# Moving the two-input elementwise work of the last token blocks from GpSimd to VectorE, with two of each eight unit pairs multiplied plainly

## The chip, the cores and the metric

The kernel runs on one core of a Trainium2 chip. The metric is the device time of one execution in microseconds (us). TensorE (PE in the profile, PEld for its weight loads) multiplies, VectorE (DVE), ScalarE (ACT) and GpSimd (POOL) work elementwise, and SyncE (SP) issues most transfers.

## The reference, cut to what matters

The first part is a spectral mixing of `x` (4 sequences of 3008 positions, 256 channels): a real FFT along the sequence, a complex 256x256 product with bias, a soft threshold, and the inverse FFT. Its 12032 rows of 256 values then go through a feed-forward network with 2048 hidden units:

```python
def _moe_ref(x, w_in, w_out, alpha):
    h = x @ w_in
    g = np.maximum(h, 0.0) + alpha * np.minimum(h, 0.0)
    return (g @ w_out).astype(np.float32)
```

The change concerns only the feed-forward network on the last 3072 of the 12032 rows, and the preparation of its weights.

## The kernel before, in words

Each fp32 operand of a matmul is split into two parts, `hi` (rounded, made by ScalarE) and `lo` (the rest, `x - hi`, made by VectorE or GpSimd), and each product is three matmuls: hi·hi, lo·hi, hi·lo. TensorE's order is the order of the program; so is that of every other engine (`manual_schedule`).

The first 24 chunks of up to 384 tokens go through the main loop, `l1_step` and `l2_step`, one hidden block of 128 units at a time; the second-layer product of a step is issued `LAG` = 3 steps behind its first-layer product. The last 3072 tokens are six blocks (`NS2` = 6) of `SC` = 512 tokens. Their hidden units go in `PR` = 8 pairs of 128-unit blocks, so there are 48 steps. Step k issues the first layer of pair k (`s_l1`) and then the second layer of pair k-2 (`s_l2`, `SLAG` = 2).

`s_l1` makes the two hidden blocks of the pair, 6 matmuls of 512 columns each, in two buffers of `ps_h`; ScalarE takes the Relu of the negative (`sq`), and a VectorE instruction, scalar_tensor_tensor, completes the activation from `sq` and `ps_h` and so frees the `ps_h` buffer.

In five of the six blocks `s_l2` replaces the 2x2 block product of a pair (two unit blocks x two token halves against two unit blocks x two channel halves, 8 products) by seven products of sums. It needs sums of the activations (`t`), with their `hi` (`h`) and `lo` (`l`) parts, those of the plain quarters (`dh`, `dl`, three quarters in one 768-element instruction), and sums of the output weights (`sw_a`, `sw_b`), which `w_full`, `w_sums` and `w_split` prepare during the last 28 main steps. Seven products accumulate over the eight pairs in three PSUM tiles `a`, `b`, `c` and in `o_last`; `s_out` combines them after the eighth pair, and `s_turn` transposes and stores. The sixth block is multiplied plainly (`z_parts`, `z_l2`, 8 products).

Work tiles rotate over two buffers by tag, so a `dh` of pair k can be written only when TensorE has read that of pair k-2, and the two `ps_o` tiles and `o_last` of a block must be emptied by `s_out` before the next block's first `s_l2` may write them. Between some steps `s_dmm` (16 matmuls, L611) and `s_dpart` (ScalarE and VectorE splits of its result, L139 and L142) make the input rows of the next block.

Of the kernel before, what the change touches and what calls it, by code (L numbers as in the profile page):

```python
# [9 lines left out]
F32 = mybir.dt.float32  # L10
F32R = mybir.dt.float32r
# [82 lines left out]
def fft_mix_moe(ctx, tc, x, w_r, w_i, b_r, b_i, w_in, w_out, alpha, la, rb, lc, rd, lf, cf, sel, out):  # L94
# [38 lines left out]
    def f(t):  # L133
        return t.bitcast(F32)
# [202 lines left out]
    xt = {}  # L337
# [401 lines left out]
    def w_full(p):  # L739

        h, m = divmod(4 * p, FH)
        w = wo_h[h][:, m:m + 4]
        t = work.tile([128, 4, C], F32, tag="xt", name="wo_f")
        G.tensor_tensor(out=t, in0=f(w[:, :, 0]), in1=f(w[:, :, 1]), op=ALU.add)
        wf.append(t)

    def w_sums(p):

        t = wf.pop().rearrange("p (r j) (c h) -> p j h r c", j=2, h=2)
        s = work.tile([128, 4, 2, 128], F32, tag="xt", name="wo_s")  # L750
        G.tensor_tensor(out=s[:, 0], in0=t[:, 0, 1], in1=t[:, 1, 1], op=ALU.add)
        G.tensor_tensor(out=s[:, 1], in0=s[:, 0], in1=t[:, 0, 0], op=ALU.subtract)
        G.tensor_tensor(out=s[:, 2], in0=t[:, 0, 0], in1=t[:, 0, 1], op=ALU.subtract)
        G.tensor_tensor(out=s[:, 3], in0=t[:, 1, 0], in1=s[:, 1], op=ALU.subtract)
        wf.append(s)

    def w_split(p):
        s = wf.pop()
        a, b = (t[:, :, 2 * p:2 * p + 2] for t in sw["all"])
        A.activation(out=a[:, 0:4], in_=s, func=AF.Copy)  # L760
        V.tensor_tensor(out=a[:, 4:6], in0=s[:, 0:2], in1=f(a[:, 0:2]), op=ALU.subtract)
        V.tensor_tensor(out=b, in0=s[:, 2:4], in1=f(a[:, 2:4]), op=ALU.subtract)
# [4 lines left out]
    def s_l1(n, t):  # L767
        yh, yl = yt[CC + n]
        q = work.tile([128, 2, SC], F32, tag="xt", name="sq")
        for j in range(2):  # L770
            m = 2 * t + j
            ps = ps_h.tile([128, SC], F32, tag="h", name="ps_h")
            k = 0
            for ct in range(CT):
                for w, a in ((0, yh), (0, yl), (1, yh)):
                    PE.matmul(ps, wi_h[m // FH][:, w, ct, 128 * (m % FH):128 * (m % FH) + 128], a[:, ct],  # L776
                              start=(k == 0), stop=(k == 3 * CT - 1))
                    k += 1
            A.activation(out=q[:, j], in_=ps, func=AF.Relu, scale=-1.0)
            V.scalar_tensor_tensor(out=q[:, j], in0=q[:, j], scalar=beta_s[:, m:m + 1], in1=ps,  # L780
                                   op0=ALU.mult, op1=ALU.add)
        if n == NS2 - 1:
            z_parts(t, q)
            return
        q = q.rearrange("p j n -> p (j n)")
        b12, b11, b22, b21 = (q[:, HS * k:HS * k + HS] for k in range(4))
        dh = work.tile([128, 3 * HS], F32R, tag="Xh", name="dh")
        dl = work.tile([128, 3 * HS], F32R, tag="Xl", name="dl")
        t3 = work.tile([128, 2, HS], F32, tag="zst", name="t3")
        t1 = work.tile([128, 2, HS], F32, tag="bt", name="t1", bufs=3)  # L790
        h3 = work.tile([128, 2, HS], F32R, tag="xh", name="h3")
        l3 = work.tile([128, 2, HS], F32R, tag="Yh", name="l3")
        h1 = work.tile([128, 2, HS], F32R, tag="xl", name="h1")
        l1 = work.tile([128, 2, HS], F32R, tag="Yl", name="l1")
        A.activation(out=dh, in_=q[:, HS:], func=AF.Copy)  # L795
        V.tensor_tensor(out=t3[:, 0], in0=b22, in1=b12, op=ALU.subtract)
        V.tensor_tensor(out=t3[:, 1], in0=t3[:, 0], in1=b11, op=ALU.add)
        G.tensor_tensor(out=dl, in0=q[:, HS:], in1=f(dh), op=ALU.subtract)  # L798
        for k, b in enumerate((b22, b21)):
            V.tensor_tensor(out=t1[:, k], in0=b, in1=t3[:, 1], op=ALU.subtract)  # L800
        A.activation(out=h3, in_=t3, func=AF.Copy)
        A.activation(out=h1, in_=t1, func=AF.Copy)
# [49 lines left out]
    def s_l2(n, t):  # L852
        if t == 0:
            sa[n] = [ps_o.tile([128, 2, HS], F32, tag="o", name="ps_o") for _ in range(2)] \
                + [ps_f.tile([128, 2, HS], F32, tag="f", name="ps_o")]
        a, b, c = sa[n]
        b11, b22, b21, t3, t2, t1, t4 = sg.pop((n, t))
        r, z = t == 0, t == PR - 1

        def block(j, h):  # L860
            m = 2 * t + j
            w = wo_h[m // FH][:, m % FH].rearrange("p w (c h) -> p w h c", h=2)
            return w[:, 0, h], w[:, 1, h]

        s1, s2, s3, s4 = ([x[:, t] for x in sw[k]] for k in range(4))
        prods = [(block(0, 0), b11, a[:, 0], r, False), (block(1, 0), b21, a[:, 1], False, z),
                 (s4, b22, b[:, 0], r, False), (s3, t3, b[:, 1], False, z),
                 (s2, t2, c[:, 0], r, False), (s1, t1, c[:, 1], False, z),
                 (block(1, 1), t4, o_last[:, 0], r, z)]
        for (wh, wl), (gh, gl), o, first, last in prods:  # L870
            PE.matmul(o, wh, gh, start=first, stop=False)
            PE.matmul(o, wl, gh, start=False, stop=False)
            PE.matmul(o, wh, gl, start=False, stop=last)

    so = {}

    def s_out(n):
        a, b, c = sa.pop(n)
        e = [work.tile([128, HS], F32, tag="q", name="se", bufs=3) for _ in range(3)]
        u = [work.tile([128, HS], F32, tag="gh", name="su", bufs=4) for _ in range(3)]  # L880
        c1 = work.tile([128, 2, HS], F32, tag="Yt", name="c1", bufs=1)
        c2 = work.tile([128, 2, HS], F32, tag="Yc", name="c2", bufs=1)
        A.activation(out=e[0], in_=a[:, 0], func=AF.Copy)
        A.activation(out=e[1], in_=b[:, 0], func=AF.Copy)
        A.activation(out=e[2], in_=c[:, 1], func=AF.Copy)
        V.tensor_tensor(out=c1[:, 1], in0=a[:, 1], in1=e[0], op=ALU.add)
        V.tensor_tensor(out=u[0], in0=c[:, 0], in1=e[0], op=ALU.add)
        V.tensor_tensor(out=u[1], in0=b[:, 1], in1=u[0], op=ALU.add)
        V.tensor_tensor(out=c2[:, 1], in0=o_last[:, 0], in1=u[1], op=ALU.add)
        G.tensor_tensor(out=u[2], in0=u[0], in1=e[2], op=ALU.add)  # L890
        G.tensor_tensor(out=c1[:, 0], in0=u[2], in1=e[1], op=ALU.add)
        G.tensor_tensor(out=c2[:, 0], in0=u[1], in1=e[2], op=ALU.add)
        so[n] = c1, c2

    def s_turn(n):
# [55 lines left out]
    with tc.manual_schedule():  # L951
# [100 lines left out]
        def at(i, fn, *args, when=todo):  # L1052
            when.setdefault(i, []).append((fn, args))
# [157 lines left out]
```

## Time and profile before

| quantity | value |
|---|---|
| median of three runs | 1458.29 us (1456.98 to 1461.1) |
| the profiled execution's own time | 1457.62 us |
| its span, first to last instruction | 1455.8 us |
| mean granted TensorE clock | 0.985 of 2.4 GHz |
| busy over the span: TensorE, VectorE, ScalarE, GpSimd | 96%, 64%, 51%, 37% |

The shares are means over stages with different limits. TensorE is busy all of 200 to 1000 us; from about 1115 to 1411 us, where the five seven-product blocks are computed, it is not. A busy time in the trace counts an instruction that holds its engine while it waits for a memory port.

### The profile page before, as it was taken

What the parts mean: (1) busy time and instruction counts of PE and PEld (TensorE: products, weight loads), DVE (VectorE), ACT (ScalarE), POOL (GpSimd) and SP (SyncE); (2) the same over time, 40 slices, a digit from 0 to 9 for tenths busy, and PEclk for the clock granted to TensorE, in tenths of its full rate; (3) what the DMA queues carried; (4) which work ended last, traced back from release to release, by engine and by line L of the source; (5) the groups of instructions that cost most, each with busy time, mean ns of one, the idle gap of its engine ahead of it and who ended that gap; (6) DMA issues with size and microseconds to landing.
All of it is one profiled execution on the core that took longest, in us unless ns stands there. A gap on an engine that the chain in (4) does not pass through costs nothing.

```text
span 1455.8 us, 25407 instructions
## 1 busy us (share of the span) xinstructions
PE 1391.5 (96%) x9640; PEld 1325.2 (91%) x9640; DVE 929.7 (64%) x1579; ACT 738.0 (51%) x1528; POOL 533.0 (37%) x539
## 2 busy tenths in 40 slices
PE   8999999999999999999999999999998888788898
PEld 5979999999999999999999999999988777677788
DVE  2758756666644446666665566656565888888874
ACT  3556554455455654544466554444545444444453
POOL 4855722223221222222212222232463554454551
PEclk9999999999999999999999999999999999999999
DMA  9954131110112321111223210111010001101001
GB/s 237 247 166 138 55 105 59 59 52 30 52 41 75 88 80 44 40 50 51 73 80 108 63 47 27 59 53 51 30 31 16 21 1 37 25 2 26 6 10 30
DMA packets 72452, 89.68 MB, mean 62 GB/s; under 512 B 22043, under 2 KB 54782, under 8 KB 72329
## 3 DMA queue, kind: packets, MB, share of 16 engines
q1 hardware_dynamic: 63743, 76.74, 18.0%
q0 software_dynamic: 5168, 8.02, 2.1%
q10 hardware_dynamic: 3418, 3.29, 0.7%
q8 instruction: 76, 1.25, 0.4%
q14 instruction: 47, 0.39, 0.1%
HBM read 50.49 MB, written 34.34 MB: 58 GB/s over the span
## 4 chain that ended last, share of the span: by engine, by line
PE 78%; DVE 13%; ACT 4%; issue 3%; DMA 1%; POOL 0%; SPq 0%; ACTq 0%; DVEq 0%; POOLq 0%
PE ps_h L672 25%; PE ps_o L710 6%; PE ps_o L711 6%; PE ps_o L709 6%; PE ps_m L486 5%; PE ps_h L776 5%; PE ps_b L426 3%; DVE t L800 3%; PE o_last L711 3%; PE ps_d L611 3%; PE o_last L709 3%; PE o_last L710 3%; DVE sq L780 3%; PE ps_m L473 3%; DVE l L804 2%
## 5 line engine op out<-in xcount | busy, mean ns | idle before, releaser
L672 PE MATMUL ps_h<-yh,w 128*128 128x384 f32 (+1 forms) x1472 | 431.5, 335 | 4.2 <-DVE q L679 4.1
L684 POOL TENSOR_TENSOR gl<-q,gh 128x384 fp32r<-128x384 f32 (+1 forms) x187 | 193.2, 1033 | 577.1 <-ACT gh L683 527.0
L679 DVE SCALAR_TENSOR_TENSOR q<-q,beta_s,ps_h 128x384 f32<-128x384 f32 (+1 forms) x384 | 230.8, 601 | 234.4 <-ACT q L678 232.3
L683 ACT ACTIVATE gh<-q 128x384 fp32r<-128x384 f32 (+1 forms) x384 | 198.3, 516 | 276.0 <-DVE q L679 272.4
L672 PEld LDWEIGHTS ps_h<-yh,w 128*128 128x128 f32 x1472 | 271.1, 189 | 8.2 <-DVE q L679 4.8
L672 PE MATMUL ps_h<-yl,w 128*128 128x384 f32 (+1 forms) x736 | 243.5, 331 | 0.0
L678 ACT ACTIVATE q<-ps_h 128x384 f32<-128x384 f32 (+1 forms) x384 | 182.5, 475 | 117.9 <-PE ps_h L672 103.0
L711 PE MATMUL ps_o<-w,gl 128*128 128x256 f32 x768 | 216.4, 282 | 3.0 <-POOL gl L684 3.0
L710 PE MATMUL ps_o<-w,gh 128*128 128x256 f32 x768 | 216.9, 282 | 0.0
L709 PE MATMUL ps_o<-w,gh 128*128 128x256 f32 x768 | 216.1, 281 | 0.0
L776 PE MATMUL ps_h<-yh,w 128*128 128x512 f32 x384 | 138.1, 422 | 35.3 <-DVE sq L780 35.3
L684 DVE TENSOR_TENSOR gl<-q,gh 128x384 fp32r<-128x384 f32 (+1 forms) x197 | 120.5, 612 | 66.4 <-ACT gh L683 62.7
L711 PEld LDWEIGHTS ps_o<-w,gl 128*128 128x128 f32 x768 | 146.0, 190 | 3.9 <-POOL gl L684 3.7
L710 PEld LDWEIGHTS ps_o<-w,gh 128*128 128x128 f32 x768 | 145.9, 190 | 0.0
L709 PEld LDWEIGHTS ps_o<-w,gh 128*128 128x128 f32 x768 | 144.7, 188 | 0.0
L672 PEld LDWEIGHTS ps_h<-yl,w 128*128 128x128 f32 x736 | 139.3, 189 | 1.4
L798 POOL TENSOR_TENSOR dl<-sq,dh 128x768 fp32r<-128x768 f32 x40 | 82.2, 2056 | 136.0 <-ACT dh L795 101.4
L776 PEld LDWEIGHTS ps_h<-yh,w 128*128 128x128 f32 x384 | 77.5, 202 | 56.0 <-DVE sq L780 39.8
L711 PE MATMUL o_last<-w,gl 128*128 128x256 f32 x352 | 100.7, 286 | 0.0
L709 PE MATMUL o_last<-w,gh 128*128 128x256 f32 x352 | 100.3, 285 | 0.0
L710 PE MATMUL o_last<-w,gh 128*128 128x256 f32 x352 | 100.3, 285 | 0.0
L800 DVE TENSOR_TENSOR t<-sq,t 128x256 f32<-128x256 f32 x80 | 99.2, 1281 | 1.4
(194 smaller groups left out, 2840.4 us busy)
## 6 DMA issues: line engine op xcount, KB each, us to landing
zt<-zd SPq DMA_DIRECT2D x32, 384.0 KB
ad<-ast SPq DMA_DIRECT2D x48, 192.0 KB
bt<-ad SPq DMA_DIRECT2D x72, 128.0 KB
zd<-zst SPq DMA_DIRECT2D x36, 256.0 KB
xt<-in_x SPq DMA_DIRECT2D x21, 320.0 KB
cw_s<-in_moe_w_in SPq DMA_DIRECT2D x8, 512.0 KB
cw_s<-in_moe_w_out SPq DMA_DIRECT2D x8, 512.0 KB
out<-os SPq DMA_DIRECT2D x26, 128.0 KB
```

Source lines behind the costliest of these rows:

```text
L486: PE.matmul(p, a[:, k:k + 128], mix[i][:, w, ct], start=(n == 0), stop=(n == 3 * CT - 1))
L672: PE.matmul(ps, wi_h[m // FH][:, w, ct, 128 * (m % FH):128 * (m % FH) + 128], a[:, ct, 0:n], start=(k == 0), stop=(k == 3 * CT - 1))
L678: A.activation(out=q, in_=ps, func=AF.Relu, scale=-1.0)
L679: V.scalar_tensor_tensor(out=q, in0=q, scalar=beta_s[:, m:m + 1], in1=ps, op0=ALU.mult, op1=ALU.add)
L683: A.activation(out=hi, in_=q, func=AF.Copy)
L684: (V if LOS[(2 * m + c) % len(LOS)] and fill or not fill and (m + c) % 2 else G).tensor_tensor(out=lo, in0=q, in1=f(hi), op=ALU.subtract)
L709: PE.matmul(a, hi[:, t], w[:, 0], start=(i, k) in first, stop=False)
L710: PE.matmul(a, hi[:, t], w[:, 1], start=False, stop=False)
L711: PE.matmul(a, lo[:, t], w[:, 0], start=False, stop=(i, k) in last)
L776: PE.matmul(ps, wi_h[m // FH][:, w, ct, 128 * (m % FH):128 * (m % FH) + 128], a[:, ct], start=(k == 0), stop=(k == 3 * CT - 1))
L798: G.tensor_tensor(out=dl, in0=q[:, HS:], in1=f(dh), op=ALU.subtract)
L800: V.tensor_tensor(out=t1[:, k], in0=b, in1=t3[:, 1], op=ALU.subtract)
```

## The change

All elementwise work with two tensor inputs in the tail leaves GpSimd for VectorE, except one subtraction of each seven-product pair (`l24`) and one `lo` part of each pair of the sixth block. The sums of a pair are taken in another order, so that two of them are one 512-element instruction in which b12 is read twice (`t13`, by a broadcast operand). In `PLAIN` pairs 1 and 2 of each eight no sums are made; `s_l2` issues the 8 plain products into the same accumulators and into the second half of `o_last`, and `s_out` adds them in, with eight VectorE instructions in place of four and three on GpSimd. The weight sums move to VectorE and are spread over two main steps. At the seam of the main loop and the tail the last two second-layer main steps are issued after the first layers of tail pairs 0 and 1, rather than all but one ahead of pair 0.

```diff
         t = work.tile([128, 4, C], F32, tag="xt", name="wo_f")
-        G.tensor_tensor(out=t, in0=f(w[:, :, 0]), in1=f(w[:, :, 1]), op=ALU.add)
-        wf.append(t)
-
-    def w_sums(p):
-
-        t = wf.pop().rearrange("p (r j) (c h) -> p j h r c", j=2, h=2)
+        V.tensor_tensor(out=t, in0=f(w[:, :, 0]), in1=f(w[:, :, 1]), op=ALU.add)
         s = work.tile([128, 4, 2, 128], F32, tag="xt", name="wo_s")
-        G.tensor_tensor(out=s[:, 0], in0=t[:, 0, 1], in1=t[:, 1, 1], op=ALU.add)
-        G.tensor_tensor(out=s[:, 1], in0=s[:, 0], in1=t[:, 0, 0], op=ALU.subtract)
-        G.tensor_tensor(out=s[:, 2], in0=t[:, 0, 0], in1=t[:, 0, 1], op=ALU.subtract)
-        G.tensor_tensor(out=s[:, 3], in0=t[:, 1, 0], in1=s[:, 1], op=ALU.subtract)
-        wf.append(s)
+        wf.extend((t.rearrange("p (r j) (c h) -> p j h r c", j=2, h=2), s))
+
+    def w_sums(p, k):
+
+        t, s = wf
+        x, y, op = ((t[:, 0, 1], t[:, 1, 1], ALU.add), (s[:, 0], t[:, 0, 0], ALU.subtract),
+                    (t[:, 0, 0], t[:, 0, 1], ALU.subtract), (t[:, 1, 0], s[:, 1], ALU.subtract))[k]
+        V.tensor_tensor(out=s[:, k], in0=x, in1=y, op=op)
...
         dh = work.tile([128, 3 * HS], F32R, tag="Xh", name="dh")
         dl = work.tile([128, 3 * HS], F32R, tag="Xl", name="dl")
-        t3 = work.tile([128, 2, HS], F32, tag="zst", name="t3")
-        t1 = work.tile([128, 2, HS], F32, tag="bt", name="t1", bufs=3)
-        h3 = work.tile([128, 2, HS], F32R, tag="xh", name="h3")
-        l3 = work.tile([128, 2, HS], F32R, tag="Yh", name="l3")
-        h1 = work.tile([128, 2, HS], F32R, tag="xl", name="h1")
-        l1 = work.tile([128, 2, HS], F32R, tag="Yl", name="l1")
+        h13 = work.tile([128, 2, HS], F32R, tag="xh", name="h13")
+        l13 = work.tile([128, 2, HS], F32R, tag="Yh", name="l13")
         A.activation(out=dh, in_=q[:, HS:], func=AF.Copy)
-        V.tensor_tensor(out=t3[:, 0], in0=b22, in1=b12, op=ALU.subtract)
-        V.tensor_tensor(out=t3[:, 1], in0=t3[:, 0], in1=b11, op=ALU.add)
-        G.tensor_tensor(out=dl, in0=q[:, HS:], in1=f(dh), op=ALU.subtract)
-        for k, b in enumerate((b22, b21)):
-            V.tensor_tensor(out=t1[:, k], in0=b, in1=t3[:, 1], op=ALU.subtract)
-        A.activation(out=h3, in_=t3, func=AF.Copy)
-        A.activation(out=h1, in_=t1, func=AF.Copy)
-        G.tensor_tensor(out=l3, in0=t3, in1=f(h3), op=ALU.subtract)
-        V.tensor_tensor(out=l1, in0=t1, in1=f(h1), op=ALU.subtract)
-        sg[n, t] = [(dh[:, HS * k:HS * k + HS], dl[:, HS * k:HS * k + HS]) for k in range(3)] \
-            + [(h[:, k], l[:, k]) for h, l in ((h3, l3), (h1, l1)) for k in range(2)]
+        d = [(dh[:, HS * k:HS * k + HS], dl[:, HS * k:HS * k + HS]) for k in range(3)]
+        if t in PLAIN:
+            A.activation(out=h13[:, 0], in_=b12, func=AF.Copy)
+            V.tensor_tensor(out=dl, in0=q[:, HS:], in1=f(dh), op=ALU.subtract)
+            V.tensor_tensor(out=l13[:, 0], in0=b12, in1=f(h13)[:, 0], op=ALU.subtract)
+            sg[n, t] = d + [(h13[:, 0], l13[:, 0])]
+            return
+        t13 = work.tile([128, 2, HS], F32, tag="zst", name="t13")
+        t24 = work.tile([128, 2, HS], F32, tag="bt", name="t24", bufs=3)
+        h24 = work.tile([128, 2, HS], F32R, tag="xl", name="h24")
+        l24 = work.tile([128, 2, HS], F32R, tag="Yl", name="l24")
+        V.tensor_tensor(out=t13, in0=q[:, HS:3 * HS].rearrange("p (k n) -> p k n", k=2),
+                        in1=b12.unsqueeze(1).to_broadcast([128, 2, HS]), op=ALU.subtract)
+        V.tensor_tensor(out=t24[:, 0], in0=b22, in1=t13[:, 0], op=ALU.add)
+        V.tensor_tensor(out=dl, in0=q[:, HS:], in1=f(dh), op=ALU.subtract)
+        V.tensor_tensor(out=t24[:, 1], in0=b21, in1=t24[:, 0], op=ALU.subtract)
+        A.activation(out=h13, in_=t13, func=AF.Copy)
+        A.activation(out=h24, in_=t24, func=AF.Copy)
+        V.tensor_tensor(out=l13, in0=t13, in1=f(h13), op=ALU.subtract)
+        G.tensor_tensor(out=l24, in0=t24, in1=f(h24), op=ALU.subtract)
+        sg[n, t] = d + [(h[:, k], l[:, k]) for h, l in ((h13, l13), (h24, l24)) for k in range(2)]
...
+        def run(prods):
+            for (wh, wl), (gh, gl), o, first, last in prods:
+                PE.matmul(o, wh, gh, start=first, stop=False)
+                PE.matmul(o, wl, gh, start=False, stop=False)
+                PE.matmul(o, wh, gl, start=False, stop=last)
+
+        if t in PLAIN:
+            b11, b22, b21, b12 = sg.pop((n, t))
+            run([(block(j, h), g, o, False, False) for h, bs, o in (
+                (0, (b11, b21), a[:, 1]), (0, (b12, b22), b[:, 0]),
+                (1, (b11, b21), o_last[:, 0]), (1, (b12, b22), o_last[:, 1])) for j, g in enumerate(bs)])
+            return
+        b11, b22, b21, t1, t3, t2, t4 = sg.pop((n, t))
+        run([(block(0, 0), b11, a[:, 0], r, False), (block(1, 0), b21, a[:, 1], False, z),
+             (s4, b22, b[:, 0], r, False), (s3, t3, b[:, 1], False, z),
+             (s1, t1, c[:, 1], r, False), (s2, t2, c[:, 0], False, z),
+             (block(1, 1), t4, o_last[:, 0], r, z)])
...
         A.activation(out=e[0], in_=a[:, 0], func=AF.Copy)
-        A.activation(out=e[1], in_=b[:, 0], func=AF.Copy)
-        A.activation(out=e[2], in_=c[:, 1], func=AF.Copy)
+        A.activation(out=e[1], in_=c[:, 1], func=AF.Copy)
+        A.activation(out=e[2], in_=o_last[:, 1], func=AF.Copy)
         V.tensor_tensor(out=c1[:, 1], in0=a[:, 1], in1=e[0], op=ALU.add)
         V.tensor_tensor(out=u[0], in0=c[:, 0], in1=e[0], op=ALU.add)
-        V.tensor_tensor(out=u[1], in0=b[:, 1], in1=u[0], op=ALU.add)
-        V.tensor_tensor(out=c2[:, 1], in0=o_last[:, 0], in1=u[1], op=ALU.add)
-        G.tensor_tensor(out=u[2], in0=u[0], in1=e[2], op=ALU.add)
-        G.tensor_tensor(out=c1[:, 0], in0=u[2], in1=e[1], op=ALU.add)
-        G.tensor_tensor(out=c2[:, 0], in0=u[1], in1=e[2], op=ALU.add)
+        V.tensor_tensor(out=u[1], in0=e[2], in1=e[1], op=ALU.subtract)
+        V.tensor_tensor(out=u[2], in0=u[0], in1=e[1], op=ALU.subtract)
+        V.tensor_tensor(out=u[0], in0=b[:, 1], in1=u[0], op=ALU.add)
+        V.tensor_tensor(out=c1[:, 0], in0=b[:, 0], in1=u[2], op=ALU.add)
+        V.tensor_tensor(out=c2[:, 1], in0=o_last[:, 0], in1=u[0], op=ALU.add)
+        V.tensor_tensor(out=c2[:, 0], in0=u[0], in1=u[1], op=ALU.add)
...
+    PLAIN = (1, 2)
```

The rest of the diff moves the seam and the weight sums:

```diff
         for p in range(PR // 2):
             at(i + 5 * p, w_full, p)
-            at(i + 5 * p + 1, w_sums, p)
-            at(i + 5 * p + 4, w_split, p)
+            for k in range(4):
+                at(i + 5 * p + 1 + k // 2, w_sums, p, k)
+            at(i + 5 * p + 3, w_split, p)
...
             put()
-            l2(min(NS, i + 1 - LAG) if i < NS - 1 else NS - 1)
-            do(todo, i)
+            l2(i + 1 - LAG)
+            if i < NS - 1:
+                do(todo, i)
...
             do(post, k)
             put()
-            if k == 0:
-                l2(NS)
+            if k < SLAG:
+                l2(NS - 2 + 2 * k)
+            if k == 1:
                 do(todo, NS - 1)
```

What stands on VectorE for one seven-product pair, in the middle of the tail. Before: `sq` is the activated pair, `t` the sums, `h` and `l` their parts; the two scalar_tensor_tensor rows (x2) complete the activation.

```order
L780 SCALAR_TENSOR_TENSOR sq<-sq,beta_s,ps_h 128x512 x2
L796 TENSOR_TENSOR t_14498<-sq 128x256
L797 TENSOR_TENSOR t_14498<-t_14498,sq 128x256
L800 TENSOR_TENSOR t_14499<-sq,t_14498 128x256 x2
L804 TENSOR_TENSOR l_14503<-t_14499,h_14502 128x512
```

The same pair now:

```order
L779 SCALAR_TENSOR_TENSOR sq<-sq,beta_s,ps_h 128x512 x2
L802 TENSOR_TENSOR t_14462<-sq 128x512
L804 TENSOR_TENSOR t_14463<-sq,t_14462 128x256
L805 TENSOR_TENSOR dl<-sq,dh 128x768
L806 TENSOR_TENSOR t_14463<-sq,t_14463 128x256
L809 TENSOR_TENSOR l_14460<-t_14462,h_14459 128x512
```

`dl` has come from GpSimd and stands between the third and the fourth sum; the `lo` part that VectorE makes is now that of the first two sums, and that of the last two (`l24`, L810) stands on GpSimd alone.

VectorE at the end of a block, where `s_out` (L886 to L892) follows the pair's last row. Before, ahead of the next block's input splits (L142):

```order
L804 TENSOR_TENSOR l_14561<-t_14557,h_14560 128x512
L886 TENSOR_TENSOR c_14599<-ps_o,se 128x256
L887 TENSOR_TENSOR su<-ps_o,se 128x256
L888 TENSOR_TENSOR su<-ps_o,su 128x256
L889 TENSOR_TENSOR c_14600<-o_last,su 128x256
```

Now, where the pair ahead of it is a plain one (its `dl` and one `lo` part, L794 and L795):

```order
L794 TENSOR_TENSOR dl<-sq,dh 128x768
L795 TENSOR_TENSOR l_14517<-sq,h_14516 128x256
L899 TENSOR_TENSOR c_14549<-ps_o,se 128x256
L900 TENSOR_TENSOR su<-ps_o,se 128x256
L901 TENSOR_TENSOR su<-se 128x256
L902 TENSOR_TENSOR su<-su,se 128x256
L903 TENSOR_TENSOR su<-ps_o,su 128x256
L904 TENSOR_TENSOR c_14549<-ps_o,su 128x256
L905 TENSOR_TENSOR c_14550<-o_last,su 128x256
L906 TENSOR_TENSOR c_14550<-su 128x256
```

Four rows of 256 elements more stand on VectorE, three of them GpSimd's before; `b` is emptied by the sixth row (L904) where before it was by the third (L888), and the pair ahead has three rows fewer.

## Rows read from the trace of the kernel before

**Rows 1.** Windows: length, busy us (instructions) by engine, granted clock, DMA share, GB/s.

```profile
600.00:800.00 200.00, 200.00 (x1475) 197.58 (x1475) 118.78 (x225) 106.74 (x232) 48.76 (x63) 1.00 0.23 70
1125.20:1411.20 286.00, 243.73 (x1416) 215.38 (x1417) 240.45 (x343) 133.80 (x246) 146.25 (x91) 0.94 0.07 17
```

**Rows 2.** Waits of TensorE, 1125.2 to 1411.2 us: total, times, longest.

```profile
PE ps_h L776 <- DVE sq L780: 35.3, 21, 3.7
PE ps_o L871 <- DVE c L886: 10.6, 4, 2.9
```

**Rows 3.** Timeline of VectorE, one tail step: start, us, instruction.

```profile
1208.09 1.39 DVE L780 SCALAR_TENSOR_TENSOR sq<-sq,beta_s,ps_h 128x512 f32<-128x512 f32 x2
1209.59 0.42 DVE L796 TENSOR_TENSOR t<-sq 128x256 f32<-128x256 f32 x1
...
1210.51 2.42 DVE L800 TENSOR_TENSOR t<-sq,t 128x256 f32<-128x256 f32 x2
1213.70 0.92 DVE L804 TENSOR_TENSOR l<-t,h 128x512 fp32r<-128x512 f32 x1 [0.78 <-ACT h L802]
1214.55 1.39 DVE L780 SCALAR_TENSOR_TENSOR sq<-sq,beta_s,ps_h 128x512 f32<-128x512 f32 x2
```

**Rows 4.** Timeline of GpSimd in the same step.

```profile
1210.55 2.09 POOL L798 TENSOR_TENSOR dl<-sq,dh 128x768 fp32r<-128x768 f32 x1 [2.94 <-ACT dh L795]
1212.60 1.48 POOL L803 TENSOR_TENSOR l<-t,h 128x512 fp32r<-128x512 f32 x1
```

**Rows 5.** Timeline of ScalarE in the same step.

```profile
1209.57 0.85 ACT L795 ACTIVATE dh<-sq 128x768 fp32r<-128x768 f32 x1 [1.39 <-PE o_last L873]
...
1213.04 0.63 ACT L802 ACTIVATE h<-t 128x512 fp32r<-128x512 f32 x1 [1.82 <-DVE t L800]
1213.58 1.07 ACT L779 ACTIVATE sq<-ps_h 128x512 f32<-128x512 f32 x2
```

**Rows 6.** VectorE by line: duration ns minimum, median, maximum.

```profile
L800 DVE TENSOR_TENSOR t<-sq,t x80: 417/1510/2125, 1120.1 to 1401.4; 128x256 f32<-128x256 f32 x80
L804 DVE TENSOR_TENSOR l<-t,h x40: 693/924/1473, 1123.2 to 1404.3; 128x512 fp32r<-128x512 f32 x40
L780 DVE SCALAR_TENSOR_TENSOR sq<-sq,beta_s,ps_h x96: 697/735/750, 1117.0 to 1442.9; 128x512 f32<-128x512 f32 x96
```

**Rows 7.** Windows of single steps that TensorE fills; the last plain.

```profile
1189.59:1194.81 5.22, 5.22 (x35) 4.73 (x34) 4.44 (x5) 1.68 (x4) 2.63 (x2) 1.00 0.00 0
1416.87:1422.49 5.62, 5.62 (x38) 5.13 (x37) 2.85 (x3) 2.35 (x5) 1.29 (x1) 1.00 0.00 0
```

**Rows 8.** The chain that ended last: the 16 matmuls of an `s_dmm`.

```profile
1108.92 1.76 PE ps_d L611 x16
```

**Rows 9.** Timeline of VectorE with input splits between two steps.

```profile
1221.00 0.24 DVE L142 TENSOR_TENSOR yl<-ps_d,yh 128x88 fp32r<-128x88 f32 x1
...
1223.21 1.40 DVE L780 SCALAR_TENSOR_TENSOR sq<-sq,beta_s,ps_h 128x512 f32<-128x512 f32 x2
```

**Rows 10.** Timeline of VectorE at a block's end (`s_out`), then transposes.

```profile
1184.96 0.41 DVE L886 TENSOR_TENSOR c<-ps_o,se 128x256 f32<-128x256 f32 x1
...
1185.73 0.42 DVE L888 TENSOR_TENSOR su<-ps_o,su 128x256 f32<-128x256 f32 x1
...
1200.36 1.41 DVE L901 STREAM_TRANSPOSE oT<-c 128x256 f32<-128x256 f32 x4
```

**Rows 11.** Timeline of TensorE: two instructions behind long waits.

```profile
1125.21 0.80 PE L776 MATMUL ps_h<-yh,w 128*128 128x512 f32 x1 [3.67 <-DVE sq L780]
...
1185.42 0.39 PE L871 MATMUL ps_o<-dh,w 128*128 128x256 f32 x1 [2.93 <-DVE c L886]
```

**Rows 12.** The chain that ended last, first-layer matmuls of a pair, slow and full clock.

```profile
1125.21 4.35 PE ps_h L776 x12
1132.04 2.75 PE ps_h L776 x12
```

**Rows 13.** Waits of TensorE, 1040 to 1114 us (weight sums are made).

```profile
PE ps_h L672 <- DVE q L679: 2.9, 4, 1.5
```

More of the change, by code (lines that the diff above doesn't have):

```diff
@@ L743, in w_full @@
         t = work.tile([128, 4, C], F32, tag="xt", name="wo_f")
-        G.tensor_tensor(out=t, in0=f(w[:, :, 0]), in1=f(w[:, :, 1]), op=ALU.add)
-        wf.append(t)
-    def w_sums(p):
-        t = wf.pop().rearrange("p (r j) (c h) -> p j h r c", j=2, h=2)
+        V.tensor_tensor(out=t, in0=f(w[:, :, 0]), in1=f(w[:, :, 1]), op=ALU.add)
         s = work.tile([128, 4, 2, 128], F32, tag="xt", name="wo_s")
-        G.tensor_tensor(out=s[:, 0], in0=t[:, 0, 1], in1=t[:, 1, 1], op=ALU.add)
-        G.tensor_tensor(out=s[:, 1], in0=s[:, 0], in1=t[:, 0, 0], op=ALU.subtract)
-        G.tensor_tensor(out=s[:, 2], in0=t[:, 0, 0], in1=t[:, 0, 1], op=ALU.subtract)
-        G.tensor_tensor(out=s[:, 3], in0=t[:, 1, 0], in1=s[:, 1], op=ALU.subtract)
-        wf.append(s)
+        wf.extend((t.rearrange("p (r j) (c h) -> p j h r c", j=2, h=2), s))
[4 more added lines that the diff above has]
+        V.tensor_tensor(out=s[:, k], in0=x, in1=y, op=op)
     def w_split(p):
-        s = wf.pop()
+        _, s = wf
+        wf.clear()
         a, b = (t[:, :, 2 * p:2 * p + 2] for t in sw["all"])
@@ L856, in s_l2 @@
         a, b, c = sa[n]
-        b11, b22, b21, t3, t2, t1, t4 = sg.pop((n, t))
         r, z = t == 0, t == PR - 1
@@ L863, in block @@
             return w[:, 0, h], w[:, 1, h]
-        s1, s2, s3, s4 = ([x[:, t] for x in sw[k]] for k in range(4))
[L866 to L873, printed above, removed]
+        def run(prods):
[10 more added lines that the diff above has]
+        b11, b22, b21, t1, t3, t2, t4 = sg.pop((n, t))
+        s1, s2, s3, s4 = ([x[:, t] for x in sw[k]] for k in range(4))
+        run([(block(0, 0), b11, a[:, 0], r, False), (block(1, 0), b21, a[:, 1], False, z),
+             (s4, b22, b[:, 0], r, False), (s3, t3, b[:, 1], False, z),
+             (s1, t1, c[:, 1], r, False), (s2, t2, c[:, 0], False, z),
+             (block(1, 1), t4, o_last[:, 0], r, z)])
     so = {}
```

## The prediction

> **What bounds the kernel now.** I read the windows by stage first. From 600 to 800 us TensorE is busy all the time at full granted clock [rows 1]; nothing elementwise can help there. From 1125.2 to 1411.2 us, the 40 steps whose second layer is a seven-product one, it is busy 243.7 of 286.0 us, and GpSimd 146 us [rows 1]. The instruction count fits 40 steps of 12 + 21 matmuls and six `s_dmm` of 16: 1416. Then the waits: TensorE waits for VectorE alone, 35.3 us for an activation that frees `ps_h` and 10.6 us for `s_out` [rows 2]. So VectorE's own order is next. One step lasts 6.46 us there (1208.09 to 1214.55), and VectorE is idle 0.78 us of it [rows 3]. The reader should see the two sums of L800: two instructions of 256 elements take 2.42 us, where L796, of the same size, takes 0.42. They last as long as GpSimd's `dl`, 1210.55 to 1212.64 [rows 4]; alone, the same instruction takes 0.417 us, and L804 takes 0.693 alone and 0.92 beside GpSimd [rows 3, 6]. So GpSimd holds up a VectorE instruction with two SBUF inputs, and this hold-up, not VectorE's own work, makes the step.
>
> What the step would take if TensorE alone set it is in the trace too: 5.22 us for 12 + 21 matmuls, 5.62 us for 12 + 24 [rows 7].
>
> **TensorE's work after the change.** 40 steps x 5.22 = 208.8; ten pairs are plain (2 of 8 in five blocks) and issue 24 matmuls instead of 21, 10 x 0.40 = 4.0 [rows 7]; six `s_dmm` of 1.76 [rows 8] are 10.6. Sum 223.4 us, against 286.0 now. The most that this stage can give is 62.6 us.
>
> **The new elementwise step.** VectorE's durations: 256 elements 0.42, 512 elements 0.69 [rows 3, 6], so 0.27 for 256 more; 768 elements, which VectorE does nowhere before, lie between 0.69 and 2.09 (GpSimd's time for it [rows 4]), and I take 0.96, one more 0.27, as both neighbours are VectorE's. An instruction that reads the one before starts about 0.03 after its end, an independent one some 0.07 before it [rows 3]. From the end of the second scalar_tensor_tensor of a pair (0): `t13` 0.10 to 0.79; third sum 0.82 to 1.24; `dl` 1.18 to 2.14 (its `dh` on ScalarE is ready at 0.94 [rows 5]); fourth sum 2.07 to 2.49; then ScalarE, 0.11 later as now (1212.93 to 1213.04), `h24` to 3.23 and, overlapped by 0.1, the two Relus of the next pair in 1.07 to 4.20 [rows 5]; VectorE's first scalar_tensor_tensor starts 3.76, the second 4.40 and ends 5.14 (0.735 each [rows 6]). `l13` (2.43 to 3.12) lies beside ScalarE's work. So this loop takes 5.14 us, where it takes 6.46 now, just under TensorE's 5.22. A broadcast operand stands nowhere before: below, `t13` costs nothing beyond its 0.69; above, it costs what L804 shows beside GpSimd, 0.92; I take 0.69, since a repeated read is still one 512-element instruction, and the 0.23 goes to the range.
>
> GpSimd keeps `l24`, 1.48 us [rows 4]: it starts at 3.36 and ends at 4.84. The next VectorE instruction with two SBUF inputs is the next `t13`, at 5.24; the scalar_tensor_tensor between reads one operand from PSUM and is as steady as 0.697 to 0.750 [rows 6]. If it did collide, the price would be up to 1.48 a pair.
>
> A plain pair has no sums: `dl` 0.97 to 1.93, one `lo` part of 0.42, and the next activation ends at about 3.6.
>
> Per block this loop has 6 x 5.14 + 2 x 3.6 = 38.0; `s_out`, now eight VectorE instructions at about 0.39 spacing (1184.96 to 1185.73 is two [rows 10]), 3.1; the four transposes, 1.41 [rows 10], of which VectorE can hide some 0.8 behind ScalarE, 0.6; the input splits 2.2 (1221.00 to 1223.21 [rows 9]) in 1.2 steps, 2.6. Sum 44.3 us, against TensorE's 223.4 / 5 = 44.7. Two loops so nearly equal do not hide each other fully: the steps differ, and each wait on either side is lost to both in part. `s_out` stands right behind a plain pair in the program, so its 3.1 us meet a step that needs 3.6 instead of 5.14; that is why I charge only about 1.1 us a block to what is left of the waits. I take 229 us for the stage: a gain of 57.
>
> What else issues is unchanged: SP's transfers stand in the same order.
>
> **The seam.** TensorE now waits 3.67 us before pair 2 and then starts at half clock [rows 11]: its 12 matmuls take 4.35 instead of 2.75 us [rows 12]. The 1.6 lie inside the 286. With two main steps moved behind pairs 0 and 1 TensorE has work while the first pair's sums are made. I take 3 us off; bounds 0 and 3.7.
>
> **The weight sums.** Four times, 1024 + 4 x 256 elements come to VectorE: by the slope above 1.2 + 4 x 0.42 = 2.9 us each, 11.6 in all, in steps that TensorE bounds. TensorE loses 2.9 us there now [rows 13], part of it through the same hold-up. The cover is VectorE's idle time in the main loop (119 of 200 us busy [rows 1]); around these sums it runs short for a few steps. I take 0; bounds 2.9 won and 4 lost.
>
> **The sum.** 1457.6 (the profiled execution's own time) - 57 - 3 = 1397.6. The median of the runs shown stands 0.7 higher: 1398 us.
>
> **A rule against it.** VectorE is busy 84% of the stage (240.45 of 286.00 [rows 1]), ScalarE 47%. The Trainium skill, Perfetto Trace Analysis, section Optimizing Scalar/DVE Operations, says that work may be moved from a saturated VectorE to ScalarE or GpSimd; the change goes the other way. The same section warns that the two share a read port, so that such a move may not help; rows 4 and 6 bear that half out, 2.09 against 0.417 us. By the first half the time would be that of the third rival.
>
> **The rivals.**
> 1. The block's end is the new wait. `b` is emptied by `s_out`'s sixth instruction, not its third, and TensorE needs it six matmuls after `a`. If the four ends cost what they cost now, 2.93 us and a half-clock loss of 1.6 [rows 11, 12], and 1.6 for four more instructions, the stage takes 223.4 + 4 x 6.1 = 248: 1417 us. For it: eight instructions in a row ahead of the next activation. Against it: the plain pair ahead of them. Chance 0.12.
> 2. The elementwise loop stays the bound by its hand-offs or by collisions with `l24`. With 0.1 more at each of five hand-offs a block takes 47.3 and the stage 237: 1406. With a collision in each pair, 6.62 a pair, 266: 1435. But a `t13` that waits for `l24` shifts the next `l24` as well, and from there the loop is 4.8 us long, shorter than TensorE's, so it would not repeat itself. Chance 0.08.
> 3. VectorE is saturated: L800's 2.08 are its own time. Then a pair takes 5.14 + 1.66 = 6.8, a block 54.3, the stage 271.5: 1441 us. Against it: 0.417 alone [rows 6]. Chance 0.05.
> 4. Slower: the clock. Behind its long waits TensorE ran at 1.2 GHz for a while, and the stage's granted clock is 0.94 [rows 1, 11]. If it were at the lower of its two levels throughout, each step would double to 10.4 and the time be about 1600 us; it decides when the mean step passes (286.0 - 14.6) / 40 = 6.8, that is with 30% of TensorE's work at half clock. Against it: 200 us of uninterrupted work at 1.00 [rows 1]. Chance 0.03.
>
> **How the numbers follow.** My forecast, TensorE setting the pace, has 0.70: 1388 to 1408. Low end: 62.6 and 3.7 and 2.9 won, 1389, and one more for the clock. The high end takes in the first rival and the cheap half of the second: 1417. Left out are collisions, saturation, the slow clock, and 0.02 for what I don't see. This kernel's runs differ by about 0.3%, so less than that cannot be told from no change. Faster 0.95, same 0.02, slower 0.03.
>
> **What would show it.** Right: in the tail GpSimd has one 1.48 us instruction in 30 of 40 pairs; no VectorE sum takes 2 us; `dl` takes 0.96; TensorE's waits there fall from 46 us to below 10 and its granted clock to 1.00; the mean step is 5.6 to 5.8 us. Wrong: `dl` or `t13` stretched beside `l24`; waits of TensorE for `s_out` of 3 us or more at each block's end; new waits of 1 us or more in the steps with weight sums.

## The result and the profile after

| quantity | before, same chip | after |
|---|---|---|
| median | 1457.63 us (4 runs, 1456.33 to 1461.1) | 1399.35 us (4 runs, 1397.42 to 1399.61) |
| ratio, 95% interval | | 0.9594 [0.9575, 0.9613] |
| profiled execution, its span | 1457.62, 1455.8 us | 1399.11, 1397.3 us |
| stage of the five seven-product blocks (40 steps) | 286.04 us | 229.27 us |

The forecast was 1398 us for the time and 229 us for the stage. The stage is measured from the first matmul of pair 2's first layer (1125.21 before [rows 11], 1123.50 after) to that of pair 42; behind it both kernels take 44.6 us. The window of the stage after, with the columns of [rows 1]:

```profile
1123.50:1352.80 229.30, 225.73 (x1449) 204.47 (x1448) 181.36 (x329) 124.39 (x238) 38.90 (x31) 1.00 0.09 22
```

TensorE is busy 225.7 of 229.3 us at the full granted clock. GpSimd's busy time went from 146 to 39 us, and VectorE's did not rise by what it took over: it fell from 240 to 181. TensorE's waits in the stage, 46 us in [rows 2], are 3.4 now:

```profile
PE ps_o L871 <- DVE c L904: 1.6, 2, 0.8
PE ps_h L775 <- DVE sq L779: 1.6, 1, 1.6
PE ps_o L871 <- DVE c L899: 0.2, 1, 0.2
```

One pair on VectorE's timeline, against [rows 3]:

```profile
1189.56 1.41 DVE L779 SCALAR_TENSOR_TENSOR sq<-sq,beta_s,ps_h 128x512 f32<-128x512 f32 x2 [0.65 <-ACT sq L778]
1191.00 0.69 DVE L802 TENSOR_TENSOR t<-sq 128x512 f32<-128x512 f32 x1
1191.80 0.42 DVE L804 TENSOR_TENSOR t<-sq,t 128x256 f32<-128x256 f32 x1
1192.14 0.95 DVE L805 TENSOR_TENSOR dl<-sq,dh 128x768 fp32r<-128x768 f32 x1
1193.01 0.42 DVE L806 TENSOR_TENSOR t<-sq,t 128x256 f32<-128x256 f32 x1
1193.35 0.68 DVE L809 TENSOR_TENSOR l<-t,h 128x512 fp32r<-128x512 f32 x1
1194.70 0.75 DVE L779 SCALAR_TENSOR_TENSOR sq<-sq,beta_s,ps_h 128x512 f32<-128x512 f32 x1 [0.67 <-ACT sq L778]
```

From one pair's start to the next, 1189.56 to 1194.70, are 5.14 us (6.46 before): VectorE does one more 768-element instruction in it and is done sooner. GpSimd's one instruction of a pair:

```profile
1189.12 1.29 POOL L810 TENSOR_TENSOR l<-t,h 128x512 fp32r<-128x512 f32 x1 [4.39 <-ACT h L808]
```

It ends at 1190.41, beside the scalar_tensor_tensors and ahead of `t13` at 1191.00. The two scalar_tensor_tensors beside it take 1.41 us together, where 1.39 were taken beside an idle GpSimd [rows 3, 4]; all 96 of the tail take 0.70 to 0.75 each, as before [rows 6]. VectorE and GpSimd by line, duration in ns minimum, median, maximum:

```profile
L804 DVE TENSOR_TENSOR t<-sq,t x30: 424/425/428, 1119.8 to 1342.7; 128x256 f32<-128x256 f32 x30
L805 DVE TENSOR_TENSOR dl<-sq,dh x30: 949/952/961, 1120.2 to 1343.0; 128x768 fp32r<-128x768 f32 x30
L806 DVE TENSOR_TENSOR t<-sq,t x30: 415/418/420, 1121.1 to 1343.9; 128x256 f32<-128x256 f32 x30
L810 POOL TENSOR_TENSOR l<-t,h x30: 1284/1295/1307, 1122.2 to 1345.2; 128x512 fp32r<-128x512 f32 x30
```

A sum of 256 elements, which in [rows 6] took 417 to 2125 ns, takes 415 to 428 now.

What is left above TensorE's own work, 229.27 - 223.4 = 5.9 us, stands mostly at three of the four block ends. The first-layer matmuls of successive pairs start 5.22 us apart (5.62 in a plain step) where nothing is lost, but 6.73, 7.06 and 6.66 there, which is 4.8 in all; the fourth end takes 5.33.

The stage gave 56.8 us. The profiled execution was 58.5 faster in all, and the rest is three terms: the opening, whose instructions are the same in both, was 2.95 us later (its first `s_dmm` at 107.69, before at 104.75); set against that, the stretch with the weight sums (1028 to 1109 us before) gave 1.3 and the seam 3.4. TensorE still waits in the steps with weight sums, 2.4 us in all against 2.9 [rows 13], 1.6 of it in one wait at a place where it did not wait before (1025 to 1112 us, after):

```profile
PE ps_h L672 <- DVE q L679: 2.4, 3, 1.6
```

### The profile page after: what moved, and what is told of

The parts are those of the page before. It is cut to its first block, busy times and chain, and to the rows that moved or that the text cites. A ratio compares the mean times of both kernels' runs of the same rounds, so it can differ in the third digit from the quotient of the medians.

```text
span 1397.3 us, 25329 instructions
## 1 busy us (share of the span) xinstructions
PE 1375.3 (98%) x9670; PEld 1316.4 (94%) x9670; DVE 873.9 (63%) x1589; ACT 728.1 (52%) x1518; POOL 401.0 (29%) x454
## 4 chain that ended last, share of the span: by engine, by line
PE 86%; DVE 6%; ACT 3%; issue 2%; DMA 1%; SPq 0%; ACTq 0%; POOL 0%; DVEq 0%
PE ps_h L672 25%; PE ps_h L775 8%; PE ps_o L710 6%; PE ps_o L711 6%; PE ps_o L709 6%; PE ps_m L486 6%; PE ps_d L611 3%; PE ps_b L426 3%; PE o_last L711 3%; PE o_last L709 3%; PE o_last L710 3%; PE ps_m L473 3%; PE ps_o L871 1%; PE ps_o L872 1%; PE ps_o L873 1%
## 5 line engine op out<-in xcount | busy, mean ns | idle before, releaser
L672 PEld LDWEIGHTS ps_h<-yh,w 128*128 128x128 f32 x1472 | 271.0, 189 | 7.3 <-DVE q L679 3.8
L684 DVE TENSOR_TENSOR gl<-q,gh 128x384 fp32r<-128x384 f32 (+1 forms) x197 | 115.9, 589 | 66.4 <-ACT gh L683 64.6
L775 PE MATMUL ps_h<-yh,w 128*128 128x512 f32 x384 | 128.0, 394 | 1.9 <-DVE sq L779 1.7
L810 POOL TENSOR_TENSOR l<-t,h 128x512 fp32r<-128x512 f32 x30 | 38.9, 1296 | 191.2 <-ACT h L808 173.8
L775 PEld LDWEIGHTS ps_h<-yh,w 128*128 128x128 f32 x384 | 72.1, 188 | 16.8 <-DVE sq L779 2.5
L779 DVE SCALAR_TENSOR_TENSOR sq<-sq,beta_s,ps_h 128x512 f32<-128x512 f32 x96 | 68.2, 742 | 22.0 <-ACT sq L778 21.8
```

The lines of the kernel that those rows point to most:

```text
L684: (V if LOS[(2 * m + c) % len(LOS)] and fill or not fill and (m + c) % 2 else G).tensor_tensor(out=lo, in0=q, in1=f(hi), op=ALU.subtract)
```

## The experiments

Theory: GpSimd's two-input instructions held up VectorE's, and that made the 6.46 us loop. Rival: VectorE was short of time, and the change pays by having less to do. Each kernel is the changed one with the edit shown. Times are medians, ratios are to the kernel before on the same chip, and "loop" is the distance from one pair's first scalar_tensor_tensor to the next pair's.

### One instruction back on GpSimd

```diff
-V.tensor_tensor(out=dl, in0=q[:, HS:], in1=f(dh), op=ALU.subtract)
+G.tensor_tensor(out=dl, in0=q[:, HS:], in1=f(dh), op=ALU.subtract)
```

> One row of the change undone: `dl` (768 elements) goes back to GpSimd in every pair of the five blocks, all else as changed. Theory (GpSimd's two-input instructions hold up VectorE's): `dl` lasts 2.1 us from about 1.1 us after the activation, the fourth sum waits inside it until about 3.2, and a seven-product pair takes 5.85 us instead of 5.14, a plain one 4.6 instead of 3.6; a block 50.6, the stage 253 instead of 229: 1423 us. Rival (VectorE's own busy time decides, fewer and longer rows were the gain): VectorE is relieved of 0.95 us a pair, and the time is 1399 or less.

Measured: 1419.46 us, ratio 0.9744 [0.9728, 0.9759]; stage 250.98, loop 5.86. VectorE has less to do and the stage is 21.7 us longer. VectorE's timeline, then GpSimd's:

```profile
1197.65 0.42 DVE L804 TENSOR_TENSOR t<-sq,t 128x256 f32<-128x256 f32 x1
1198.11 1.97 DVE L806 TENSOR_TENSOR t<-sq,t 128x256 f32<-128x256 f32 x1
```

```profile
1197.97 1.84 POOL L805 TENSOR_TENSOR dl<-sq,dh 128x768 fp32r<-128x768 f32 x1 [1.64 <-PE ps_h L775]
```

L804 and L806 are of one size. L806 comes 0.14 us behind GpSimd's start and ends 0.27 behind its end (1199.81): it waits for the whole of it. The rival falls.

### All rows of a pair as before

The four sums in their old order, `dl` and the first `lo` part on GpSimd; seam, weights and plain pairs stay changed.

```diff
-V.tensor_tensor(out=t13, in0=q[:, HS:3 * HS].rearrange("p (k n) -> p k n", k=2),
-                in1=b12.unsqueeze(1).to_broadcast([128, 2, HS]), op=ALU.subtract)
...
+V.tensor_tensor(out=t3[:, 0], in0=b22, in1=b12, op=ALU.subtract)
+V.tensor_tensor(out=t3[:, 1], in0=t3[:, 0], in1=b11, op=ALU.add)
+G.tensor_tensor(out=dl, in0=q[:, HS:], in1=f(dh), op=ALU.subtract)
...
```

> The seven-product pairs have their rows of before (four separate sums on VectorE, `dl` and the first `lo` part on GpSimd); plain pairs, `s_out`, seam and weight sums as changed. Theory: 6 x 6.46 + 2 x 3.6 + 6.3 = 52.3 us a block, 261 for the stage: 1431 us, so that more than half of the 58 us gain is gone. Rival (the plain pairs and the block's end did most of it): below 1410 us. Rival (the moved rows did all): 1441 us or more.

Measured: 1430.24 us, ratio 0.9818 [0.9801, 0.9834]; stage 260.93, loop 6.46 as before. So of the 56.8 us of the stage the new rows of a pair are 31.7 (260.93 - 229.27); the plain pairs and the new `s_out`, with the better state behind the seam, are the other 25, which the runs below divide only in part.

### An extra GpSimd instruction: two inputs, one input, one input later

```diff
+xs_ = work.tile([128, TC], F32R, tag="gl", name="extra", bufs=4)
+G.tensor_tensor(out=xs_, in0=q[:, 0:TC], in1=q[:, TC:2 * TC], op=ALU.add)
 V.tensor_tensor(out=t13, in0=q[:, HS:3 * HS].rearrange("p (k n) -> p k n", k=2),
```

In the second kernel the added line is `G.tensor_scalar(out=xs_, in0=q[:, 0:TC], scalar1=1.0, scalar2=0.0, op0=ALU.mult, op1=ALU.add)`, in the third the same on `q[:, TC:2 * TC]`. `TC` is 384; nothing reads the result.

> As changed, with one GpSimd instruction more in each seven-product pair: a tensor_tensor of 384 elements on two SBUF operands, issued as the sums begin, whose result nothing reads. GpSimd is idle there, so its time alone costs nothing. Theory (it holds up VectorE's two-input instructions): about 1.0 us long as in the main loop; the third sum, alone 0.42, waits for its end and takes about 1.2; a pair takes 5.95 instead of 5.14, a block 49, the stage 246: 1416 us. Rival (VectorE is only as slow as its own work): no VectorE row gets longer, 1399 us.

> The same place and size as the extra two-input instruction, but a tensor_scalar with one SBUF operand, whose result nothing reads. Theory, if the hold-up belongs to GpSimd's two-input form: 1399 to 1400 us, no VectorE row longer. If any GpSimd work in SBUF holds VectorE up: the third sum is stretched by most of its length (some 0.5 to 0.7 us for 384 elements), and the time is 1408 us or more.

> The changed kernel with one added GpSimd instruction in each seven-product pair: a one-input operation on 128x384 of the second half of q, whose result nothing reads. It needs the pair's second activation, so that it comes due only when both scalar_tensor_tensors are nearly through and stands beside VectorE's sums, where the earlier one-input run did not. If the hold-up belongs to two-input forms on GpSimd: the third sum stays at 0.42 us, time 1397 to 1400 us. If any GpSimd work on SBUF holds VectorE's two-input sums: one sum of each such pair is stretched by some 0.4 to 0.7 us, the time about 1404 to 1412 us.

Measured: two inputs 1411.98 us, ratio 0.9678 [0.9662, 0.9694], stage 242.52; one input 1396.81, 0.9573 [0.9558, 0.9587], stage 228.57; one input later 1398.5, 0.959 [0.9564, 0.9616], stage 230.55. The second settles nothing: its instruction needs only the pair's first activation and ran at 1194.65, ahead of `t13` at 1195.25, beside no two-input row. In the third it stands beside them. The third kernel by line (the sum, the extra instruction), then the extra instruction of the second by line, which shows its length alone:

```profile
L806 DVE TENSOR_TENSOR t<-sq,t x30: 605/608/611, 1118.4 to 1342.9; 128x256 f32<-128x256 f32 x30
L803 POOL TENSOR_SCALAR extra<-sq x30: 915/1009/1013, 1117.8 to 1342.3; 128x384 fp32r<-128x384 f32 x30
```

```profile
L803 POOL TENSOR_SCALAR extra<-sq x30: 511/512/517, 1118.1 to 1339.8; 128x384 fp32r<-128x384 f32 x30
```

And the two timelines where they meet, VectorE's and GpSimd's, in the third kernel:

```profile
1190.30 0.69 DVE L804 TENSOR_TENSOR t<-sq 128x512 f32<-128x512 f32 x1
1191.02 0.61 DVE L806 TENSOR_TENSOR t<-sq,t 128x256 f32<-128x256 f32 x1
```

```profile
1190.35 1.01 POOL L803 TENSOR_SCALAR extra<-sq 128x384 fp32r<-128x384 f32 x1 [0.63 <-DVE sq L779]
```

In the third kernel both branches of the expectation missed in part. The time is the one written for "only two-input forms hold VectorE up", but all 30 sums are stretched, 0.42 to 0.61, so a one-input GpSimd instruction does hold VectorE up. The yardstick is the second kernel, whose loop is 5.06 and not 5.14: in the kernels with an added instruction the sum follows `t13` by 0.03 us, and in the changed kernel, where a semaphore instruction of VectorE's stands between them, by 0.10. So the 0.19 make the loop 5.25, a little over TensorE's 5.22, and cost the stage 2.0 us against the second kernel, 1.3 against the changed one. The hold-up is mutual and in turn: GpSimd's 0.51 us instruction starts 0.05 behind `t13`, ends 0.37 behind its end and so takes 1.01; the next sum starts while it runs and ends 0.27 behind it. With two inputs it is the same, longer: the extra instruction takes 1.52 and the sum 1.13, and ends 0.29 behind it (1198.36 + 1.13 against 1197.68 + 1.52). The loop there is 5.76 and the stage 13 us longer than the changed kernel's, somewhat less than the 5.95 and 17 expected. VectorE's row and GpSimd's in that kernel:

```profile
1198.36 1.13 DVE L806 TENSOR_TENSOR t<-sq,t 128x256 f32<-128x256 f32 x1
```

```profile
1197.68 1.52 POOL L803 TENSOR_TENSOR extra<-sq 128x384 fp32r<-128x384 f32 x1 [0.64 <-DVE sq L779]
```

### No plain pairs

```diff
-    PLAIN = (1, 2)
+    PLAIN = ()
```

and `s_out` without the terms of `o_last[:, 1]`.

> No pair is plain: all eight of a block are seven-product pairs, `s_out` has one copy and one VectorE instruction fewer; all else as changed. Theory (without plain pairs the elementwise loop is the longer one): 8 x 5.14 + 2.7 for `s_out` + 0.6 + 2.6 = 47.0 us a block, 235 for the stage instead of 229: 1405 us, and waits of TensorE for activations come back. Rival (TensorE sets the pace with room to spare): ten times 0.40 us of matmuls less, 1395 us.

Measured: 1401.44 us, ratio 0.9621 [0.9606, 0.9637], stage 234.45. The stage is as expected (235), its form is not; the time lies 3.6 below the 1405 expected, the opening of this execution was 3.2 earlier than the changed kernel's (first `s_dmm` at 104.53), and the ratio's interval overlaps the changed kernel's, so the stage tells more than the time. Most steps take 5.22, and the loss over TensorE's own 219.4 (208.8 + 10.6) stands mostly at the block ends, where pairs start 8.85, 8.04 and 7.92 us apart, and just behind them. `s_out` stands behind a whole seven-product pair there. Beside the new rows, then, the plain pairs are worth 5.2 us of stage. The longest of TensorE's waits in the stage:

```profile
PE ps_o L871 <- DVE c L898: 2.9, 2, 1.5
PE ps_h L775 <- DVE sq L779: 2.7, 2, 2.5
PE ps_o L871 <- DVE c L902: 1.8, 3, 0.7
```

### Plain pairs in another place, and one in place of two

```diff
-    PLAIN = (1, 2)
+    PLAIN = (4, 5)
```

and `PLAIN = (1,)` in the other kernel.

> The changed kernel with the plain products in pairs 4 and 5 of each eight instead of 0 and 1: the same products and sums in number, TensorE's work the same, but the pairs at the block's end have sums now. Theory: plain pairs pay by where they stand, since around the block's end VectorE also has the output's sums and the input splits, and the run without plain pairs lost its time there: the stage is 236 to 238 us in place of 229.3, the time about 1406 to 1408 us. Rival (only VectorE's load over a whole block counts): stage 229 us, time 1398 to 1400 us.

> The changed kernel with one plain pair in eight (pair 1) in place of two. TensorE's work in the stage falls by about 2 us to 221.4; VectorE's rows in a block come to seven loops of 5.14 us, one of 3.6 and the output's sums. If these fill the block, VectorE sets a stage of 228 to 232 us and the time is 1397 to 1402 us, no better than the changed kernel; if the waits at the block's end go with pair 0's sums instead, as in the run without plain pairs, the stage is nearer to 234 and the time about 1403 us.

(These two texts misnumber the pairs: the code counts them from 0, the changed kernel has 1 and 2 plain, and the sums that come back in the second are those of pair 2.) Measured: plain 4 and 5, 1409.07 us, ratio 0.9661 [0.9639, 0.9683], stage 238.35; plain 1 alone, 1397.82, 0.9581 [0.9564, 0.9598], stage 228.02. With the same work on every engine, two plain pairs in the middle of a block are worth 9.1 us less: 6.1 of it stands in the four steps at block ends, 1.0 in the stage's first step. At the block's end with plain 4 and 5, VectorE from the pair's last scalar_tensor_tensor to `s_out`'s first row (L899):

```profile
1168.80 0.74 DVE L779 SCALAR_TENSOR_TENSOR sq<-sq,beta_s,ps_h 128x512 f32<-128x512 f32 x1
...
1171.92 0.68 DVE L809 TENSOR_TENSOR l<-t,h 128x512 fp32r<-128x512 f32 x1
1173.05 0.43 DVE L899 TENSOR_TENSOR c<-ps_o,se 128x256 f32<-128x256 f32 x1 [0.45 <-ACT se L896]
```

and with plain 1 alone:

```profile
1167.28 1.41 DVE L779 SCALAR_TENSOR_TENSOR sq<-sq,beta_s,ps_h 128x512 f32<-128x512 f32 x2 [0.67 <-ACT sq L778]
1169.66 0.96 DVE L794 TENSOR_TENSOR dl<-sq,dh 128x768 fp32r<-128x768 f32 x1 [0.97 <-ACT dh L790]
1170.54 0.42 DVE L795 TENSOR_TENSOR l<-sq,h 128x256 fp32r<-128x256 f32 x1
1170.87 0.42 DVE L899 TENSOR_TENSOR c<-ps_o,se 128x256 f32<-128x256 f32 x1
```

`s_out` starts 3.5 us after the pair's activation in the one (1169.54 to 1173.05) and 2.2 in the other (1168.69 to 1170.87). The last 0.45 of the 3.5 is a wait for ScalarE's copy (`se`), which stands behind the copies of the pair's sums in ScalarE's order. One plain pair ahead of `s_out` does it; the second costs TensorE 2.0 us (5 x 0.40) and gives 0.8 of it back. The time of this version cannot be told from the changed kernel's on the same chip (0.9578 below).

### The block's end rearranged

`u[1]`, which no PSUM tile waits for, goes to just ahead of `s_out`'s last row, and the next block's input splits come two steps later.

```diff
-                first += 3
+                first += 5
```

> An attempt at a faster version: in `s_out` the one instruction that touches no accumulator is moved behind those that empty `b` and `o_last`, and the input splits that stood right behind `s_out` come two steps later. Theory (what TensorE still loses in the stage lies at the block's ends, 1.8 us at one with splits, 0.8 at two waits for `b`): 2 to 3 us less, 1396.5 to 1397.5. Rival (the splits cost the same wherever they stand): 1399.

Measured: 1396.47 us, ratio 0.9576 [0.9559, 0.9593], stage 228.93, 0.34 less than the changed kernel's. The step that took 7.06 takes 5.69, but two later ones take 7.35 and 6.58: the splits cost VectorE the same wherever they stand. That was the rival. The time alone would have spoken for the theory (1396.5 to 1397.5); its profiled execution has the earliest opening of all, first `s_dmm` at 104.30.

### The old seam, and the weight sums on GpSimd

```diff
-            l2(i + 1 - LAG)
+            l2(min(NS, i + 1 - LAG) if i < NS - 1 else NS - 1)
...
-        V.tensor_tensor(out=s[:, k], in0=x, in1=y, op=op)
+        G.tensor_tensor(out=s[:, k], in0=x, in1=y, op=op)
```

> The last main steps stand again where they stood (all but one second-layer step ahead of pair 0, the last behind it), all else as changed. Theory: TensorE's wait before pair 2 comes back in part, 2 to 3.4 us: 1401 to 1403 us. Rival (with the shorter pair the old order is as good): 1399 us.

> The weight sums go back to GpSimd in their old steps, all else as changed. Theory (I priced this part of the change at nothing, within 2.9 won and 4 lost): within 2 us of 1399. The two traces, set against each other at the same instruction, let this part win about 1.3 us: then 1400 to 1401. If VectorE's shortage beside the sums were the larger effect: 1397.

These are two kernels. Measured: old seam 1402.62 us, ratio 0.9622 [0.9605, 0.964]; weights on GpSimd 1399.3, 0.9588 [0.9574, 0.9603]. Set against the opening's start, the old seam makes the fourth tail pair 4.1 us later, 2.5 of it ahead of pair 2 and 1.6 inside the stage. TensorE waits 2.71 us and is behind it at a mean granted clock of 0.92, over 22 us that begin with the tail (the changed kernel's 21.7 us there have 1.00):

```profile
1125.66 0.50 PE L775 MATMUL ps_h<-yh,w 128*128 128x512 f32 x1 [2.71 <-DVE sq L779]
```

```profile
1116.20:1138.20 22.00, 19.29 (x104) 16.53 (x103) 13.16 (x21) 9.84 (x19) 1.26 (x1) 0.92 0.20 54
```

With the weight sums on GpSimd the stretch from the `s_dmm` at 1030 us to the one at 1110 lasts 80.71 us, as before (80.72); in the changed kernel it lasts 79.44. The trace shows this 1.3 us, the timed runs do not resolve it.

### The changed kernel once more

> The changed kernel itself once more, as the yardstick on this chip for the three others: 1397 to 1400 us, a ratio of 0.958 to 0.961 to the kernel before, the stage 229.3 us long; only the opening's start may differ by up to 3 us from the profile shown.

Measured: 1397.61 us (1394.65 to 1399.17), ratio 0.9578 [0.9557, 0.9598]; stage 229.18, first `s_dmm` at 106.10 where the profile above has 107.69. So the stages reproduce to 0.1 us and the openings do not.

## Why the prediction was right

**What bounded the kernel.** Right, and shown from both sides: one instruction back on GpSimd brings the stretched sum back with 21.7 us of stage, and an unneeded one puts a stretched sum where there was none. The Trainium skill, SBUF — State Buffer, section Who interferes with whom, states it: a VectorE instruction with two SBUF inputs contends with a GpSimd instruction that reads SBUF, the shared ports are an exclusive lock, and the order of issue decides which of the two waits. The trace agrees (a 256-element sum ends 0.27 to 0.29 us behind GpSimd's end in three kernels, whatever GpSimd's form). The scalar_tensor_tensor, with one operand in PSUM, is not stretched beside GpSimd (0.75 us at most).

**The loop.** 5.14 predicted, 5.14 measured; `dl` 0.96 and 0.95, a broadcast operand for nothing (0.69). Its inside was off by twice 0.07 us, and the two cancel: `t13` starts 0.03 behind the activation in place of 0.10, and the next sum 0.10 behind `t13` in place of 0.03. The mean step is 5.73, in the 5.6 to 5.8 given.

**The block.** The charge of 1.1 us a block, a choice more than a working, came out as 5.9 / 5 = 1.2; but it is not spread: three block ends hold 4.8 of it. The reason given, that `s_out` meets a shorter step behind a plain pair, is what moving the plain pairs showed. Of the first rival, waits of 2.9 us at each end, two of 0.8 are left for `b`, and the granted clock is 1.00 in the steps at all four ends.

**The seam and the weights.** 3.4 for 3 predicted; 2.5 of it comes with the order of the steps, by the run with the old seam, and the rest, by difference, with the pair's shorter rows. 1.3 won where 0 was taken, inside its bounds of 2.9 and -4. One sign of being wrong did show, a new wait of over 1 us beside the weight sums (1.6). The waits there are less in sum even so, 2.4 for 2.9; where the other 0.8 of the 1.3 comes from stays open.

**`l24`.** Mis-sized: 1.48 predicted, 1.30 measured. The row taken [rows 4] starts at 1212.60, while VectorE's second L800 sum runs to 1212.93 [rows 3], so it most likely holds a wait for that sum. It cost nothing, since nothing waits for `l24`.

**The sum.** 1457.6 - 56.8 - 3.4 - 1.3 + 2.95 = 1399.1, the profiled execution's own time. The opening was no term of the prediction; its scatter, 104.3 to 107.9 over the profiled executions, is as large as the seam. That the time came within 1.4 us of the forecast is therefore in part luck; the stage, which reproduces to 0.1 us, is the better witness.

**The rivals.** Saturation (1441) is excluded by VectorE's busy time, which fell by 59 us while it took rows over; collisions with `l24` did not occur; the clock went up, not down.

## What to carry to other kernels

Where two engines share a port, read an instruction's shortest duration against its median: if it is often several times longer and always ends just behind the other engine's, its busy time is waiting, and moving work onto the engine that looks fuller can shorten the loop. A step made cheaper pays where something irregular stands next to it: two plain pairs at the block's end were worth 9 us more than the same two in its middle, and one did as well as two. With a loop 0.08 us below the pace of TensorE, look for what is left at the seams and block ends, not in the loop.

## What the runs showed of the hardware that was not expected

A one-input GpSimd instruction on SBUF holds up VectorE's two-input instructions as a two-input one does, only for less long (the sum takes 0.61 us against 1.13, alone 0.42). And VectorE holds up GpSimd in the same way, so that GpSimd's durations in such a trace are too long as well: 0.51 us alone and 1.01 behind a `t13`, for the same 384 elements. The hold-up is still in the changed kernel where it costs nothing: in the sixth block, in both kernels, VectorE's `lo` part of 512 elements has a median of 1.36 us (0.69 alone [rows 6]) beside GpSimd's of 1.29, and TensorE's steps there are 5.62 us in both.
